# Two attention and feed-forward layers on one core: keys and values made before later queries, the passes of the opening reordered, VectorE's share of the softmax given out by another rule

## Chip, core and metric

One core of a Trainium2 chip. The metric is the device time of one execution in microseconds. A profile's span is the time from the first to the last instruction, about 1.8 us less. All timed runs and profiles named here are in the fast state. A ratio is the mean of one kernel's fast runs over the mean of the other's in the same rounds, so it is not quite the ratio of the medians quoted beside it. In the profiles PE is TensorE (matmuls) and PEld its weight loads, ACT is ScalarE, DVE VectorE and POOL GpSimd; ACTIVATE is the ScalarE instruction that computes exponentials. PSUM is the memory that the matmuls here write; a score tile fills one bank of it. PEclk is the granted clock of TensorE, 1.00 being full; a stretch of half clock is one that the profile records at 0.5.

## The reference, cut to what matters

```python
# 2048 rows of 448, bfloat16; 16 heads of 28; hidden width 1792
x = x + attention(layernorm(x), wqkv, wo)        # full softmax, no mask
x = x + mlp(layernorm(x), w1, b1, w2, b2)        # relu(h)**2
x = x + attention(layernorm(x), wqkv, wo)        # the same weights again
x = x + mlp(layernorm(x), w1, b1, w2, b2)
```

A score tile in this document is 128 keys x 512 columns (two key blocks for 256 queries of one head); there are 1024 a layer, 2048 in all. Every one needs an exponential.

## The kernel before

The kernel doesn't fix its instruction order by hand. While the program is built, a small planner simulates the engines with given durations and priorities, and emits instructions in the order that comes out. A number in it can therefore move work anywhere. The order is fixed when the kernel runs.

```python
BB = 0.85
CUT0 = (0, 2, 4, 8, 12, 16)
LEAD = 60                     # no VectorE tile before this group of scores
V_LATE = 3.0
LAT = {"PE": 0.22, "ACT": 0.22, "DVE": 0.10, ...}   # planner's latencies, us
...
# row statistics of a layer norm, with the duration that the planner assumes
o = Op("DVE", 0.80, fn, deps=deps)
...
# may a score tile be taken from ScalarE and given to VectorE?
def apart(i, now, us, soon=SOON):
    ...
    if pl.load(SPAN, "DVE") > (BB if l == 0 and qb == len(blocks[0]) - 1
                               or l == 1 and units[i][0] < bridged else BUSY):
        return None
    return j
...
# one group of scores: three banks of PSUM for one ACTIVATE
if bank_free(o.start) and next_at(js[-1] + 1):
    j = apart(at[0], o.start, us)            # a fourth tile, in a bank of its own
elif len(us) == 3 and THIRD:
    own = False
    j = apart(at[0], o.start, us[:2], 0.0)   # VectorE takes the third bank
...
# TensorE repeats score matmuls where the plan sees room, so that it isn't idle
for i in list(range(4)) * (again + 1):
    ...
```

A tile that VectorE takes is computed with six instructions (one read from PSUM, four polynomial steps, one power of two). "Chain" below is what follows the attention of 256 rows: output projection, layer norm, feed-forward, and in layer 0 the keys, values and queries of layer 1. The two banks that aren't score buffers serve the chains, the accumulation of the attention output, and the fourth tiles.

The softmax here doesn't subtract the row's maximum and nothing guards it: scores larger than these inputs give would overflow.

## Time and profile before

| | before |
|---|---|
| median of the first 3 runs | 905.57 us |
| ScalarE: three-tile and two-tile ACTIVATEs | 592 and 76 |
| tiles on VectorE | 120 |
| first exponential starts, last one ends | 12.04, 883.44 us |
| after the last exponential | 20.2 us |

The prediction shows the lines and reads them.

### The profile page before, as it was taken

The page shows a single profiled execution, that of the slowest core. Times are in us where ns is not written, and L with a number is a line of the kernel's source. Part 1 is how long each engine was busy: PE and PEld are TensorE (multiplying, and loading weights), DVE is VectorE, ACT ScalarE, POOL GpSimd, SP SyncE. Part 2 cuts the span into 40 slices and gives each one's busy share as a digit, 9 for nine tenths or more (in the row PEclk, how much of TensorE's full clock was granted, in tenths as well). Part 3 has the DMA queues.
Part 4 walks back from the last instruction along what each step waited for, and adds up shares of the span by engine and source line. Part 5 has one row for each costly group of instructions (what it writes and reads, how often), then busy time and mean ns, then how long its engine had stood idle before and what let it go on. Part 6 is the DMA issues. An engine that isn't in the chain of part 4 may idle for free.

```text
span 903.7 us, 29597 instructions
## 1 busy us (share of the span) xinstructions
PE 833.2 (92%) x13089; PEld 464.8 (51%) x13089; DVE 779.4 (86%) x1595; ACT 876.9 (97%) x688; POOL 42.7 (5%) x100
## 2 busy tenths in 40 slices
PE   7999989899999999998999999988999999999998
PEld 4555545455454555545545454544454545545566
DVE  7845789999998999988888988989999999989864
ACT  6999999999999999999999999999999999999992
POOL 4100000000000000000000000000000000000000
PEclk9999999999999999999999999999999999999999
DMA  6200010000000000000000000011000000000100
GB/s 202 95 3 2 2 38 22 15 8 15 9 14 14 15 13 10 14 9 7 3 1 2 2 2 2 2 40 38 24 15 19 14 25 8 25 16 17 29 6 22
DMA packets 32990, 18.47 MB, mean 20 GB/s; under 512 B 17499, under 2 KB 32412, under 8 KB 32861
## 3 DMA queue, kind: packets, MB, share of 16 engines
q1 hardware_dynamic: 32860, 16.58, 6.4%
q8 instruction: 102, 1.67, 0.8%
q14 instruction: 28, 0.22, 0.1%
HBM read 14.26 MB, written 2.07 MB: 18 GB/s over the span
## 4 chain that ended last, share of the span: by engine, by line
ACT 66%; PE 14%; issue 13%; DVE 5%; DMA 1%; POOL 0%; SPq 0%; POOLq 0%; ACTq 0%
ACT pt L805 66%; PE mt L532 6%; PE sc L781 5%; PE oT L950 2%; PE mt L1138 1%; DVE K_sb L878 1%; DMA V_sb<-in_A_wqkv_dram 1%; DVE st L425 1%; DVE xn L498 1%; DVE v_h L878 1%; DVE x_sb L1044 1%; PE sc L532 0%; PE tp L471 0%; DVE K_sb L861 0%; DVE v_i L861 0%
## 5 line engine op out<-in xcount | busy, mean ns | idle before, releaser
L805 ACT ACTIVATE pt<-sc 128x1536 bf16<-128x1536 f32 (+1 forms) x668 | 866.4, 1565 | 2.2 <-PE sc L781 1.7
L781 PE MATMUL sc<-Q_sb,K_sb 32*128 32x256 bf16 (+1 forms) x5966 | 325.9, 265 | 52.7 <-ACT pt L805 47.4
L781 PEld LDWEIGHTS <-K_sb 32*128 32x128 bf16 x6102 | 160.3, 92 | 227.3 <-issue 209.0
L950 PE MATMUL oT<-pt,V_sb 128*32 128x256 bf16 (+1 forms) x4104 | 152.3, 268 | 0.6 <-DVE K_sb L974 0.2
L532 PE MATMUL mt<-xnT,w 128*128 128x256 bf16 (+1 forms) x888 | 118.2, 271 | 3.1 <-DVE r L1087 1.1
L950 PEld LDWEIGHTS <-V_sb 128*32 128x32 bf16 x4352 | 92.4, 96 | 47.5 <-issue 44.5
L878 DVE SCALAR_TENSOR_TENSOR K_sb<-K_sb 128x512 f32<-128x512 uint16 x165 | 113.1, 686 | 0.7
L532 PEld LDWEIGHTS <-w 128*128 128x128 bf16 x952 | 79.0, 98 | 37.6 <-issue 28.9
L878 DVE SCALAR_TENSOR_TENSOR v_h<-v_h,v_i 128x512 f32<-128x512 f32 x130 | 89.1, 685 | 0.4
L1087 DVE TENSOR_SCALAR r<-mt 128x512 bf16<-128x512 f32 x105 | 72.1, 687 | 14.2 <-PE mt L532 14.1
L532 PE MATMUL mt<-w,V_sb 128*128 128x448 bf16 (+1 forms) x288 | 68.6, 352 | 0.0
L447 POOL TENSOR_TENSOR ve<-mv,eps_t 128x2 f32<-128x2 f32 (+1 forms) x34 | 9.5, 280 | 843.7 <-DVE mv L426 778.5
L1138 PE MATMUL mt<-xn,ident 128*128 128x448 bf16 x133 | 45.9, 356 | 2.5 <-DVE x_sb L1044 1.3
L878 DVE SCALAR_TENSOR_TENSOR v_h<-v_i 128x512 f32<-128x512 uint16 x65 | 44.6, 686 | 0.3
L1044 DVE TENSOR_TENSOR x_sb<-x_sb,mt 128x448 bf16<-128x448 bf16 (+1 forms) x64 | 39.1, 611 | 6.3 <-PE mt L532 6.0
L425 DVE BATCH_NORM_STATS2 st<-x_sb 128x6 f32<-128x448 bf16 x64 | 39.6, 619 | 1.0 <-DMA x_sb<-in_A_x_dram 0.6
L532 PEld LDWEIGHTS <-V_sb 128*128 128x128 bf16 x302 | 25.5, 98 | 24.6 <-issue 9.1
L498 DVE TENSOR_SCALAR xn<-x_sb,mv,rstd 128x448 bf16<-128x448 bf16 x64 | 25.3, 420 | 12.9 <-POOL rstd L448 12.5
L532 PE MATMUL mt<-xnT,wq 128*128 128x256 bf16 x248 | 34.0, 274 | 0.0
L532 PE MATMUL mt<-xnT,wk 128*128 128x256 bf16 x240 | 32.9, 274 | 0.6 <-DVE xnT L483 0.4
L1091 DVE TENSOR_TENSOR V_sb<-r 128x512 bf16<-128x512 bf16 (+1 forms) x73 | 30.3, 417 | 2.3 <-ACT r L1085 1.8
L554 DVE CAST K_sb<-mt 128x512 bf16<-128x512 f32 (+1 forms) x31 | 20.8, 672 | 12.7 <-PE mt L532 12.5
(102 smaller groups left out, 790.5 us busy)
## 6 DMA issues: line engine op xcount, KB each, us to landing
rec<-scr SPq DMA_DIRECT2D x56, 128.0 KB
x_sb<-in_A_x_dram SPq DMA_DIRECT2D x8, 224.0 KB
out_dram<-x_sb SPq DMA_DIRECT2D x15, 112.0 KB
w<-in_B_w_dram SPq DMA_DIRECT2D x1, 1568.0 KB
w<-in_B_w_dram SPq DMA_DIRECT2D x1, 1344.0 KB
dn<-oT_sb SPq DMA_DIRECT2D x56, 4.0 KB
scr<-dn SPq DMA_DIRECT2D x56, 4.0 KB
V_sb<-in_A_wqkv_dram SPq DMA_DIRECT2D x1, 672.0 KB
```

Source lines behind the costliest of these rows:

```text
L425: nc.vector.bn_stats(out=st[:, :], in_=x_sb[:, t0 + j, :])
L498: nc.vector.tensor_scalar(out=xn[:, 0:D], in0=x_sb[:, t0 + j, :], scalar1=mv[0][:, j, 0:1], scalar2=ln[j], op0=ALU.subtract, op1=ALU.mult)
L532: nc.tensor.matmul(box["t"][:, c0:c0 + n], lhsT=lhsT() if callable(lhsT) else lhsT, rhs=rhs, start=a, stop=b)
L554: nc.vector.tensor_copy(out=dst, in_=src)
L781: nc.tensor.matmul(dst[k][:, i * nt * P:(i + 1) * nt * P], lhsT=K_sb[l][rows, g, (kb + i) * P:(kb + i + 1) * P], rhs=Q_sb[rows, g, t0 * P: ...
L805: t = nc.scalar.activation(out=pt[:, 0:n], in_=gbuf[gi]["sc"][:, 0:n], func=AF.Exp, scale=float(np.log(2.0)) * 2.0 ** -FRAC)
L878: nc.vector.scalar_tensor_tensor(out=box["h"], in0=box["f"] if begin else box["h"], scalar=b, in1=box["f"], op0=ALU.add, op1=ALU.mult)
L950: nc.tensor.matmul(box["t"][DHP * hh:DHP * hh + DHP, 0:n], lhsT=V_sb[l][:, kb + i, 4 * g + hh, :], rhs=p[:, c0:c0 + n], start=begin and kb ...
L1044: nc.vector.tensor_tensor(out=x_sb[:, tb, lo:hi], in0=x_sb[:, tb, lo:hi], in1=t[:, 0:hi - lo], op=ALU.add)
L1087: nc.vector.tensor_scalar(out=r[:, 0:w], in0=t[:, 0:w], scalar1=0.0, scalar2=None, op0=ALU.max)
L1091: nc.vector.tensor_tensor(out=h[:, 0:w // n, :], in0=r, in1=r, op=ALU.mult)
L1138: nc.tensor.matmul(t[:, 0:D], lhsT=ident[:, :], rhs=xns[0][:, 0:D], start=True, stop=True)
```

## The change

The intent: make all of layer 0's keys and values before the queries of later blocks; keep the normalized rows of blocks 2 to 5 in layer 1's key memory, which is still empty, so that they don't occupy the three row buffers; let VectorE take tiles early; and hold it back where the chains are behind a line of progress. The core of the diff:

```diff
-BB = 0.85
+LINES = ((280, 1312, 8.0), (1440, 2040, 7.0))
+MARGIN = 4.0
+LOW = 0.6
-CUT0 = (0, 2, 4, 8, 12, 16)
+OPENING = ((0, 0, 2), (0, 2, 4), (1, 0, 4), (0, 4, 8), (1, 4, 8), (0, 8, 12), (0, 12, 16), (1, 8, 16))
+OWN3 = 0
-LEAD = 60
+LEAD = 20
-LAT = {"PE": 0.22, "ACT": 0.22, ...}
+LAT = {"PE": 0.25, "ACT": 0.22, ...}
-        o = Op("DVE", 0.80, fn, deps=deps)
+        o = Op("DVE", 0.74, fn, deps=deps)
-            box["x"] = xtp.tile([P, NDC, QR], DT.bfloat16, name="xnT")
+            box["x"] = xtp.tile(...) if place is None else place
+   # in first_block: place=K_sb[1][:, :, (blk - 2) * QR:(blk - 1) * QR] if 2 <= blk <= 5 else None
             def queries():
+                if l == 0 and t0 >= 4:
+                    yield Op("-", 0.0, None, deps=[("V", 0, tb) for tb in range(NTB)])
+    def behind(i):
+        l = 0 if i < LINES[0][1] else 1
+        a, b, n = LINES[l]
+        return done[l] < (min(i, b) - a) / (b - a) * n * per[l] - MARGIN
-        if pl.load(SPAN, "DVE") > (BB if l == 0 and ... else BUSY):
+        if pl.load(SPAN, "DVE") > (LOW if behind(i) else BUSY):
-                if bank_free(o.start) and next_at(js[-1] + 1):
+                if OWN3 and bank_free(o.start) and next_at(js[-1] + 1):
# cut: priorities of VectorE tiles, two more limits on which tile VectorE may take,
# three more planner durations, counting of chain progress, waits that protect the rows lent to layer 1's key memory
```

More of the change, by code (lines that the diff above doesn't have):

```diff
@@ L53 @@
 V_PRIO = 6.0
-V_LATE = 3.0
+V_LATE = 3.6
+V_LAST = 1.8
+V_AGE = 5
+OWN3 = 0
+FIRST = 90
+V_FIRST = 9.2
 V_WAIT = 5.0
@@ L109, in __init__ @@
         self.need, self.got, self.more = need, [], 0.0
-LAT = {"PE": 0.22, "ACT": 0.22, "DVE": 0.10, "POOL": 0.15, "DMA": 2.0, "-": 0.0}
+LAT = {"PE": 0.25, "ACT": 0.22, "DVE": 0.10, "POOL": 0.15, "DMA": 2.0, "-": 0.0}
 class Planner:
@@ L426, in fn, with layernorm @@
             nc.vector.bn_aggr(out=mv[0][:, j, :], in_=st[:, :])
-        o = Op("DVE", 0.80, fn, deps=deps)
+        o = Op("DVE", 0.74, fn, deps=deps)
         mv[1].append(o)
         return o
-    def layernorm(t0, nt, deps_of, early=False, mv=None):
+    def layernorm(t0, nt, deps_of, early=False, mv=None, place=None):
         if mv is None:
@@ L448, in rsqrt @@
                 nc.gpsimd.tensor_tensor(out=rstd[:, a:b], in0=ve[:, a:b], in1=mhalf[:, a:b], op=ALU.pow)
-            rs = Op("POOL", 0.95 if early else 0.6, rsqrt, deps=[mv[1][b - 1]], sets=[("rs", t0 + a)] if early else ())
+            rs = Op("POOL", 0.95, rsqrt, deps=[mv[1][b - 1]], sets=[("rs", t0 + a)] if early else ())
             rss += [rs] * (b - a)
@@ L454, in take @@
         def take(e):
-            box["x"] = xtp.tile([P, NDC, QR], DT.bfloat16, name="xnT")
-        own_xt = Op("DVE", 0.0, take, acq=R_xt)
+            box["x"] = xtp.tile([P, NDC, QR], DT.bfloat16, name="xnT") if place is None else place
+        own_xt = Op("DVE", 0.0, take, acq=R_xt if place is None else None)
         yield own_xt
@@ L611, in queries @@
             def queries():
+                if l == 0 and t0 >= 4:
+                    yield Op("-", 0.0, None, deps=[("V", 0, tb) for tb in range(NTB)])
                 for a in qs:
                     yield from turned(*a)
-                yield Op("DVE", 0.0, None, deps=[last], rel=own_xt)
+                yield Op("DVE", 0.0, None, deps=[last], rel=own_xt if own_xt.res else None)
             if l == 0:
@@ L622, in first_block @@
         gate = [] if GATE[blk] is None else [GATE[blk]]
-        xnT, own_xt, ends = yield from layernorm(2 * blk, 2, lambda j: [("x", blk // 2, blk % 2), *gate, *([("xT", TILES)] if blk == 1 and XT else [])], early)
+        xnT, own_xt, ends = yield from layernorm(2 * blk, 2, lambda j: [("x", blk // 2, blk % 2), *gate, *([("xT", TILES)] if blk == 1 and XT else [])], early,
+                                            place=K_sb[1][:, :, (blk - 2) * QR:(blk - 1) * QR] if 2 <= blk <= 5 else None)
         yield from qkv(0, 2 * blk, 2, xnT, own_xt, ends, early)
@@ L632, in add_passes @@
                     passes.append((l, qb, g, range(lo, hi), lo == 0, hi == NTB))
-    for cut in zip(CUT0, CUT0[1:]):
-        if cut == (0, 2):
-            add_passes(0, [0], cut)
-        elif cut == (2, 4):
-            add_passes(0, [0], cut)
-            add_passes(0, [1], (0, 4))
-        else:
-            add_passes(0, [0, 1], cut)
+    for qb, lo, hi in OPENING:
+        add_passes(0, [qb], (lo, hi))
     for qb in range(2, len(blocks[0])):
@@ L666 @@
     held = [0]
+    done = [0.0, 0.0]
+    per = [1.6 + 7 + 5.6 + 6.0, 1.6 + 7 + 5.6]
+    def behind(i):
+        l = 0 if i < LINES[0][1] else 1
+        a, b, n = LINES[l]
+        return done[l] < (min(i, b) - a) / (b - a) * n * per[l] - MARGIN
     pending = [0]
@@ L693, in apart @@
             j = js[0] if js else j
+        if passes[units[j][0]][0] != passes[us[0][0]][0]:
+            return None
         if held[0] + 1 > min(sum(r.n for r in pd_free(units[k])) for k in (i, j)):
@@ L697, in apart @@
             return None
-        if pl.load(SPAN, "DVE") > (BB if l == 0 and qb == len(blocks[0]) - 1 or l == 1 and units[i][0] < bridged else BUSY):
+        if pl.load(SPAN, "DVE") > (LOW if behind(i) else BUSY):
             return None
@@ L821, in pd_free @@
             return (R_pd[0], *(R_pd[1:5] if qb <= 6 else R_pd[3:5]))
+        if len(norm_done.get((0, len(blocks[0]) - 1), ())) < G:
+            return tuple(R_pd[:1])
         return tuple(R_pd[:1] + R_pd[6:]) if hidden_left[0] else tuple(R_pd[:1] + R_pd[5:])
@@ L866, in a_unit @@
         yield c
-        pl.spawn(lambda now: V_LATE if now > c.end + V_WAIT else V_PRIO, a_rest(gi, c, box, unit, (b0, b1, b2, b3)))
+        pl.spawn(lambda now: V_LAST if e_now[1] - gi >= V_AGE else V_LATE if now > c.end + V_WAIT else V_PRIO if gi > FIRST else V_FIRST, a_rest(gi, c, box, unit, (b0, b1, b2, b3)))
     def a_rest(gi, c, box, unit, bs):
@@ L1011, in spread @@
                                   in_=res["t"][DH::DHP, 0:n])
-            d1 = Op("DMA", 0.5, spread, deps=[oe], lat=0.5)
+            d1 = Op("DMA", 0.5, spread, deps=[oe], lat=1.0)
             yield d1
@@ L1034, in mul @@
                                     in1=box["r"][:, 0:n], op=ALU.mult)
-        m = Op("DVE", 0.1 + n / 960, mul, deps=[r, oTn_of[l, qb][1]], rel=oe)
+        m = Op("DVE", 0.13 + n / 930, mul, deps=[r, oTn_of[l, qb][1]], rel=oe)
         yield m
@@ L1059, in chain @@
                 post=[lambda a, j=j: stats(mv, t0, j, [a])])
+            done[l] += 0.8
         yield Op("DVE", 0.0, None, deps=[a], rel=own_on)
         xnT, own_xt, ends = yield from layernorm(t0, nt, None, mv=mv)
-        own_h = Op("DVE", 0.0, None, acq=R_h[l])
+        own_h = Op("DVE", 0.0, None, acq=R_h[l], deps=[("Q", 0, g, t0 + 4) for g in range(G)] if l == 0 and qb < 4 else ())
         yield own_h
@@ L1099, in chain @@
                 relu, 0.70, [*ends, ("w1",)], True, post=[then], acq=R_r)
+            done[l] += w / 512
             for i in range(len(fcs)):
@@ L1116, in chain @@
                           (lambda a, store=store: Op("DMA", 0.5, store, deps=[a]))])
+            done[l] += 2.8
         yield Op("DVE", 0.0, None, deps=[a], rel=own_h)
@@ L1121, in chain @@
             yield from qkv(1, t0, nt, *xt2)
+            done[0] += 6.0
     def heat():
```

## The prediction

> **What bounds the kernel now.** I first read the page's busy shares and the chain that ended last, then the groups by form, then ScalarE's timeline of the opening, then busy time by stretch.
>
> ```profile
> PE 833.2 (92%) x13089; PEld 464.8 (51%) x13089; DVE 779.4 (86%) x1595; ACT 876.9 (97%) x688; POOL 42.7 (5%) x100
> ...
> ACT 66%; PE 14%; issue 13%; DVE 5%; DMA 1%; POOL 0%; SPq 0%; POOLq 0%; ACTq 0%
> ```
>
> ScalarE (ACT) is busy 97% of the span and holds two thirds of the chain. Its work is the softmax's exponentials. Three score tiles of 128x512 (or two) are one ACTIVATE:
>
> ```profile
> L805 ACT ACTIVATE pt<-sc 128x1536 bf16<-128x1536 f32 x592 | 812.9, 1612 | 2.2 <-PE sc L781 1.7 <-PE oT L950 0.2
> L805 ACT ACTIVATE pt<-sc 128x1024 bf16<-128x1024 f32 x76 | 87.4, 1197 | 0.0
> ```
>
> The columns are count, busy time, mean ns and idle time before. Neighbours overlap, so the means can't be summed. I took the distance between the ends of consecutive ACTIVATEs from the trace's records: the median is 1343 ns where the later one has three tiles and 917 ns where it has two. The difference, 426 ns, is one tile; what is left, 1343 - 3 x 426 = 65 ns (or 63 with 426.7 a tile), is the fixed cost of one. Check: 592 x 1.343 + 76 x 0.917 = 864.7, against 866.4 us busy on the page. Of the 2048 tiles, 592 x 3 + 76 x 2 = 1928 go to ScalarE; the other 120 are a polynomial on VectorE.
>
> ```profile
> core 0: us, PE busy (x) PEld busy (x) DVE busy (x) ACT busy (x) POOL busy (x), PEclk, DMA share, GB/s
> ...
> 12.00:28.00 16.00, 13.55 (x165) 7.86 (x166) 13.04 (x28) 13.63 (x13) 6.34 (x13) 1.00 0.68 211
> 28.00:60.00 32.00, 31.06 (x443) 17.46 (x444) 22.20 (x48) 32.00 (x25) 3.67 (x8) 1.00 0.03 11
> 60.00:330.00 270.00, 249.81 (x4010) 140.82 (x4004) 234.98 (x475) 269.42 (x208) 7.56 (x20) 1.00 0.05 14
> 330.00:470.00 140.00, 130.12 (x1945) 69.58 (x1942) 124.11 (x241) 139.92 (x109) 6.87 (x16) 1.00 0.03 8
> 470.00:700.00 230.00, 211.83 (x3225) 114.46 (x3222) 208.18 (x424) 229.69 (x181) 7.28 (x18) 1.00 0.05 14
> 700.00:883.00 183.00, 170.21 (x3063) 96.52 (x3061) 159.48 (x329) 183.00 (x144) 5.40 (x10) 1.00 0.07 18
> 883.00:904.00 21.00, 16.98 (x204) 12.51 (x200) 9.33 (x22) 4.41 (x8) 0.93 (x2) 1.00 0.06 19
> ```
>
> Busy time by stretch shows ScalarE full from 28 to 883 us: even the boundary between the layers (330 to 470) costs it 0.08 us. So the span is three pieces: 12.0 us before the first exponential, 871.4 from its start to the end of the last (883.4), and 20.3 of tail. The middle holds 864.7 of exponentials at their regular distance and 6.7 of anything else. Most of that 6.7 is in the opening:
>
> ```profile
> 12.04 2.79 ACT L805 ACTIVATE pt<-sc 128x1536 bf16<-128x1536 f32 x2 [0.19 <-PE sc L781]
> 14.72 0.54 ACT L580 CAST V_sb<-sc 128x448 bf16<-128x448 f32 x1
> 15.32 2.79 ACT L805 ACTIVATE pt<-sc 128x1536 bf16<-128x1536 f32 x2
> 19.05 1.45 ACT L805 ACTIVATE pt<-sc 128x1536 bf16<-128x1536 f32 x1 [0.93 <-PE sc L781]
> 20.79 0.37 ACT L552 CAST K_sb<-sc 128x256 bf16<-128x256 f32 x1 [0.30 <-PE sc L532]
> 21.55 0.53 ACT L580 CAST V_sb<-mt 128x448 bf16<-128x448 f32 x1 [0.38 <-PE mt L532]
> 22.08 4.14 ACT L805 ACTIVATE pt<-sc 128x1536 bf16<-128x1536 f32 x3
> 26.86 0.38 ACT L548 ACTIVATE Q_sb<-mt 128x256 bf16<-128x256 f32 x1 [0.65 <-PE mt L532]
> ```
>
> Between the first and the ninth exponential stand four evictions, 0.54 + 0.37 + 0.53 + 0.38 = 1.82 us, and idle times of 0.93 + 0.30 + 0.38 + 0.65 = 2.26. After 28 us all stalls that I find in the records sum to about 2 us, none over 0.43.
>
> **What the Trainium skill says.** "ScalarE: Activation LUTs", section What ACT_TABLE_LOAD costs, gives an ACTIVATE with immediate operands 186 ns + 0.833 ns per element, and an overlap of about 93 ns back to back, so 93 ns fixed. The trace agrees on the element (426 / 512 = 0.833 ns), and has 63 to 65 ns fixed; I use the trace. "Advanced Engine Details and Errata", section Bank Collisions, lets ScalarE and VectorE read PSUM at full rate at once when they are in different banks. The 76 two-tile ACTIVATEs, 75 of them beside a VectorE read of the third bank of the same buffer, keep to 917 ns, so it agrees. "SBUF — State Buffer", section Who interferes with whom, says that a VectorE tensor_scalar in a two-port mode and a GpSimd instruction exclude each other for a whole instruction. The trace fits: at 14.56 us two normalizations take 2.13 us together (420 ns each elsewhere) beside GpSimd memsets of 0.94 and 1.60 us.
>
> **The change part by part.** I compared the instruction order of both built programs.
>
> *Exponentials.* Before, 45 VectorE tiles had a bank of their own beside a full three-tile ACTIVATE, and 75 were the third bank of a score buffer. Now all are the third bank, and there are 126. ScalarE has 556 three-tile and 127 two-tile ACTIVATEs: 556 x 3 + 127 x 2 = 1922 tiles. Six fewer tiles save 6 x 0.427 = 2.56 us; 683 instead of 668 instructions cost 15 x 0.063 = 0.95. Directly: 556 x 1.343 + 127 x 0.917 = 863.2, so **-1.5 us** out of 864.7. VectorE starts at the 20th ACTIVATE instead of the 60th, which fills the stretch of 28 to 60 us where it was busy only 22.2 of 32; that stretch gets 8 tiles where it had one. The rest of the program, under the hold-back by chain progress, gives one back net.
>
> *VectorE's load.* A tile there is a read of 0.69, four steps of 0.68 and one of 0.42 us; issued back to back they stand 0.60 and 0.34 apart, so 5 x 0.60 + 0.34 = 3.3 us. Six more are +20 us; joining two pass pieces of the opening removes 4 additions of partial sums (32 to 28), -1.4. VectorE goes to about 798 us, 88%. Still under ScalarE.
>
> *Opening.* The instructions before the first exponential are the same, so 12.0 us stay. Then come five exponentials in a row, two key evictions and one of values (0.37 + 0.37 + 0.53 = 1.27 us), then exponentials without end. One eviction of 0.55 us moves from ScalarE to VectorE, and the query eviction with its wait (0.38 + 0.65 = 1.03) leaves ScalarE too. Against it, VectorE now does one row statistic (0.79), one value eviction (0.61) and one partial sum (0.41) more before it copies the transposed rows of block 1, on which the sixth exponential waits. Some of this hides in the GpSimd collision (2.13 - 0.72 = 1.4 us). I put the sixth exponential at 21 to 22 us, against 22.08. Choosing half a microsecond earlier, and 1.03 for the query: **-1.5 us**.
>
> *Early VectorE tiles.* They begin at group 19 while keys of rows 6 and 7 are due at group 22, on a VectorE that still makes them[...]. I allow **+0.5 us** for a wait there. Keeping rows in layer 1's key memory frees row buffers but removes no instruction: the order shows as many projections and transposes as before, only with another source tile.
>
> *Boundary and tail.* ScalarE had no wait at the boundary to win back. The last exponential is still a two-tile one, and the listings of VectorE and ScalarE after it match line for line: 20.3 us stay. For a fuller VectorE I allow **+0.5 us** more of small PE waits.
>
> Sum: -1.5 - 1.5 + 0.5 + 0.5 = -2.0; 905.57 - 2.0 = 903.6, and since the author's tuning should have removed some of the 2 us of small stalls, I say 903.3.
>
> **The rivals.** *A shared score bank held too long.* A score buffer is free only once both engines have read it, and shared reads go from 75 to 126. Were each late by 0.1 us, 51 x 0.1 = 5 us would come back and the time would be about 908. Against it: in the trace before, VectorE's read ended a median 0.6 us before the ACTIVATE that shares the buffer, the latest 0.16 us after, and none was followed by idle ScalarE. *VectorE becomes the bound.* At 88% in sum, parts are fuller: 90.5% in 470 to 700 now. If chains fall behind, layer 1's last keys come late and ScalarE idles at the boundary: 2 to 6 us, so 905 to 909. Against it: the hold-back exists for this, and ten percent stays free. *The opening stalls.* If early tiles delay the keys of later blocks, 2 to 4 us are lost before 60 us: 905 to 907. *It opens better than I think.* If all 4.1 us but the 1.27 of evictions go, and small stalls too, the time is about 900.5.
>
> **Range and chances.** Exponentials are counted and hardly uncertain (0.3 us). The opening is uncertain by 1.5 us either way, the later stalls by 1 to 2, more on the slow side. So 8 in 10 for 901.0 to 905.9. Two per cent is 18 us: more than everything that isn't an exponential or the unchanged ends, so faster by that much is almost excluded, and slower needs 26 ns more on each of 683 ACTIVATEs (18 / 683): 1% each.
>
> **What would show it right or wrong.** Right: 556 and 127 ACTIVATEs at the same 1343 and 917 ns, busy near 864.8; VectorE near 798; ScalarE without idle time from the sixth exponential on but for about 2 to 3 us in all; a tail of 20.3 us. The step on the opening is wrong if ScalarE's sixth exponential starts after 22.5 us, or if idle time stands near the 20th to 30th. The step on shared banks is wrong if score matmuls wait for VectorE's read, or the two-tile distance exceeds 917. All is wrong if ScalarE idles for microseconds near the layer boundary, or the tail is not 20.3.

## The result, and the profile after

903.79 us (median of 4 runs, 902.81 to 904.10), against 906.14 before in the same rounds; the ratio is 0.9969 (95%: 0.9949 to 0.9989). A later call on another occasion gave 903.20 against 906.39, ratio 0.9962. The prediction was 903.3, with a range of 901.0 to 905.9.

The page of the changed kernel: first busy time by engine, then the chain that ended last.

```profile
PE 833.8 (92%) x12828; PEld 459.2 (51%) x12828; DVE 798.2 (89%) x1628; ACT 874.6 (97%) x702; POOL 41.8 (5%) x100
...
ACT 72%; issue 13%; PE 9%; DVE 5%; DMA 1%; SPq 0%; ACTq 0%; DVEq 0%
```

VectorE rose by 18.8 us and ScalarE stayed at 97%, with more of the chain. The groups by form:

```profile
L819 ACT ACTIVATE pt<-sc 128x1536 bf16<-128x1536 f32 x556 | 776.8, 1652 | 4.1 <-PE sc L795 3.9
L819 ACT ACTIVATE pt<-sc 128x1024 bf16<-128x1024 f32 x127 | 146.0, 1235 | 0.0
```

These are the two counts of the prediction; the idle time before them nearly doubled, from 2.2 to 4.1 us. The distances between the ends of ACTIVATEs are unchanged, 1343 and 917 ns as medians. ScalarE's timeline in the opening (start, duration, what, count, and in brackets the idle time before):

```profile
11.16 5.52 ACT L819 ACTIVATE pt<-sc 128x1536 bf16<-128x1536 f32 x4 [0.19 <-PE sc L795]
17.59 1.45 ACT L819 ACTIVATE pt<-sc 128x1536 bf16<-128x1536 f32 x1 [0.91 <-PE sc L795]
19.32 0.37 ACT L559 CAST K_sb<-sc 128x256 bf16<-128x256 f32 x1 [0.28 <-PE sc L539]
19.75 0.37 ACT L559 CAST K_sb<-mt 128x256 bf16<-128x256 f32 x1
20.51 0.53 ACT L587 CAST V_sb<-mt 128x448 bf16<-128x448 f32 x1 [0.38 <-PE mt L539]
20.94 49.45 ACT L819 ACTIVATE pt<-sc 128x1536 bf16<-128x1536 f32 x38
```

From the start of the first exponential to that of the ninth it is 13.78 us, against 15.16 before (12.04 to 27.20): 1.38 less. Of these, 0.25 us are gained up to the sixth (9.78 against 10.03), and 1.13 after it, where the query eviction with its wait stood. After the sixth there is no break at all up to 70 us, though VectorE's tiles start here. The surprise is later:

```profile
400.05 2.97 ACT L819 ACTIVATE pt<-sc 128x1536 bf16<-128x1536 f32 x2 [0.28 <-PE sc L795]
404.30 1.45 ACT L819 ACTIVATE pt<-sc 128x1536 bf16<-128x1536 f32 x1 [1.28 <-PE sc L795]
406.09 4.14 ACT L819 ACTIVATE pt<-sc 128x1536 bf16<-128x1536 f32 x3 [0.34 <-PE sc L795]
```

ScalarE waits for score matmuls, and busy time by stretch suggests why: the granted clock of TensorE, PEclk, falls. (It is the first number after the five engines.) The first line is the stretch that the prediction called the boundary between the layers; there ScalarE was idle for 0.08 us before the change and is now for 2.60.

```profile
core 0: us, PE busy (x) PEld busy (x) DVE busy (x) ACT busy (x) POOL busy (x), PEclk, DMA share, GB/s
330.00:470.00 140.00, 129.02 (x1902) 69.31 (x1901) 121.79 (x231) 137.40 (x110) 5.39 (x12) 0.98 0.03 8
...
390.00:395.00 5.00, 4.25 (x90) 2.84 (x89) 5.00 (x11) 5.00 (x5) 1.06 (x4) 1.00 0.09 29
395.00:400.00 5.00, 3.51 (x64) 2.14 (x62) 5.00 (x10) 4.77 (x4) 0.00 (x0) 0.78 0.00 0
400.00:405.00 5.00, 5.00 (x41) 2.16 (x36) 2.68 (x6) 3.60 (x3) 0.00 (x0) 0.54 0.02 4
405.00:410.00 5.00, 5.00 (x95) 2.69 (x94) 1.68 (x4) 4.66 (x4) 0.00 (x0) 1.00 0.08 23
```

The clock records place one stretch of half clock at 397.8 us, 6.8 us long. I sum what each ACTIVATE after 30 us took beyond its regular distance (excesses under about 0.05 us left out) and call it late waits: 1.96 us before, 3.94 after, of which 2.4 in this stretch.

The accounts of the two profiles, 903.7 - 901.8 = 1.9 us: exponentials 864.7 - 863.2 = 1.5; opening 1.4; an earlier first exponential 0.9; a tail shorter by 0.1; less 2.0 of late waits. The pieces sum to 1.9.

### The profile page after: what moved, and what is told of

Same layout as the page of the kernel before. It is cut to its first block, busy times and chain, and to the rows that moved or that the text cites. A ratio compares the mean times of both kernels' runs of the same rounds, so it can differ in the third digit from the quotient of the medians.

```text
span 901.8 us, 29143 instructions
## 1 busy us (share of the span) xinstructions
PE 833.8 (92%) x12828; PEld 459.2 (51%) x12828; DVE 798.2 (89%) x1628; ACT 874.6 (97%) x702; POOL 41.8 (5%) x100
## 4 chain that ended last, share of the span: by engine, by line
ACT 72%; issue 13%; PE 9%; DVE 5%; DMA 1%; SPq 0%; ACTq 0%; DVEq 0%
ACT pt L819 72%; PE mt L539 4%; PE sc L795 2%; PE oT L966 1%; DVE st L432 1%; PE sc L539 1%; DMA V_sb<-in_A_wqkv_dram 1%; DVE K_sb L894 1%; DVE v_h L894 0%; DVE xn L505 0%; DVE x_sb L1060 0%; PE mt L1158 0%; DVE mv L433 0%; DVE v_i L877 0%; DVE K_sb L877 0%
## 5 line engine op out<-in xcount | busy, mean ns | idle before, releaser
L795 PEld LDWEIGHTS <-K_sb 32*128 32x128 bf16 x5840 | 156.6, 92 | 234.2 <-issue 204.2
L894 DVE SCALAR_TENSOR_TENSOR v_h<-v_h,v_i 128x512 f32<-128x512 f32 x142 | 96.9, 682 | 0.5
L877 DVE TENSOR_SCALAR v_i<-sc 128x512 int32<-128x512 f32 x71 | 48.6, 685 | 9.9 <-PE sc L795 9.3
L894 DVE SCALAR_TENSOR_TENSOR v_h<-v_i 128x512 f32<-128x512 uint16 x71 | 48.6, 685 | 0.5
L877 DVE TENSOR_SCALAR K_sb<-sc 128x512 int32<-128x512 f32 x55 | 37.6, 684 | 5.6 <-PE sc L795 5.4
L988 DVE COPY oT_sb<-oT 128x256 f32<-128x256 f32 (+1 forms) x48 | 19.0, 396 | 17.0 <-PE oT L966 16.9
L539 PE MATMUL mt<-wo,oTn 128*128 128x448 bf16 x128 | 31.6, 355 | 0.1
```

What stands on the lines that cost most here:

```text
L539: nc.tensor.matmul(box["t"][:, c0:c0 + n], lhsT=lhsT() if callable(lhsT) else lhsT, rhs=rhs, start=a, stop=b)
L795: nc.tensor.matmul(dst[k][:, i * nt * P:(i + 1) * nt * P], lhsT=K_sb[l][rows, g, (kb + i) * P:(kb + i + 1) * P], rhs=Q_sb[rows, g, t0 * P: ...
L877: t = nc.vector.tensor_scalar(out=box["i"], in0=two(src), scalar1=EXP_BIAS, scalar2=EXP_LOW, op0=ALU.add, op1=ALU.max)
L894: nc.vector.scalar_tensor_tensor(out=box["h"], in0=box["f"] if begin else box["h"], scalar=b, in1=box["f"], op0=ALU.add, op1=ALU.mult)
L988: nc.vector.tensor_copy(out=dst, in_=src)
```

## The experiments

"Ninth" is the start of the ninth exponential after that of the first; "exponentials" is three-tile count x 1.343 + two-tile count x 0.917 (and 0.490 for one tile), from the built program and the distances. Runs named a_ edit the changed kernel, b_ and bo_ the kernel before. All results were correct. The three calls (after_again to a_split, b_stats to a_best, a_own3 to a_oldorder) ran on three different chips and had 906.39, 906.17 and 906.01 us for the kernel before, so medians of different calls differ by 0.4 us from that alone.

| run | median us | ratio to before | exponentials | ninth | late waits | tail |
|---|---|---|---|---|---|---|
| before (39 runs beside the last call) | 906.01 | 1 | 864.7 | 15.16 | 1.96 | 20.2 |
| after_again | 903.20 | 0.9962 | 863.2 | 13.78 | 3.84 | 20.2 |
| a_heat | 901.72 | 0.9951 | 863.2 | 15.41* | 1.73 | 20.2 |
| a_pool | 902.67 | 0.9964 | 863.2 | 13.81 | 4.20 | 20.2 |
| a_split | 908.65 | 1.0033 | 869.4 | 15.41* | 5.04 | 20.2 |
| b_stats | 909.76 | 1.0039 | 865.4 | 13.79 | 1.91 | 24.1 |
| b_opening | 917.87 | 1.0124 | 863.5 | 16.48* | 12.59 | 23.0 |
| a_lead60 | 906.54 | 1.0004 | 866.6 | 13.78 | 0.47 | 23.0 |
| a_best | 900.49 | 0.9938 | 863.2 | 12.78 | 1.72 | 20.2 |
| a_own3 | 904.20 | 0.9982 | 862.7 | 13.78 | 4.86 | 19.9 |
| a_bb | 906.99 | 1.0008 | 863.6 | 13.78 | 3.36 | 24.5 |
| bo_own0 | 909.44 | 1.0036 | 866.1 | 17.55* | 0.84 | 22.5 |
| a_oldorder | 906.63 | 1.0003 | 865.3 | 13.78 | 2.93 | 21.9 |

(* this profile had a stretch of half clock in the opening as well.)

My theory after the result: ScalarE's count and the opening give about 3 us, and a stretch of half clock takes 2 us of it back (run 2 limits the second part to the two profiles). The rivals: the waits near 400 us are waits for VectorE's tiles; the gain in the opening comes from other parts of the change than I thought.

**1. The changed kernel again.**

> The changed kernel once more, so that the others of this call can be compared with it on one chip. Theory A (the clock dip belongs to the change's own instruction order): its profile shows again a granted clock near 0.54 between 400 and 405 us of the span, and about 3.2 us of ScalarE idle time between 376 and 407 us. Theory B (the dip was chance): a mean clock of 1.00 and less than 1 us of idle time there. The first exponential, at 12.04 us in the kernel before and 11.16 in the changed one, moves with the landing of the first weights if it is chance: anywhere from 11 to 12.2.

The half clock is there again, at 397.4 us and 6.8 us long, with similar waits (2.0 us of idle ScalarE between 376 and 408 us, where I had expected 3.2): it belongs to the program. The first exponential started at 12.15 us this time. Over all profiles it lies between 11.06 and 12.15 with the same ScalarE instructions before it. The chain of each profile begins with the transfer of the first weights, which ended at 7.72 us in the kernel before, at 6.84 in the changed one and at 7.83 this time. So the 0.9 us of the first comparison were the landing of that transfer, by chance.

**2. More score matmuls before the half clock.** The plan stays (the trace lists the same 702 ScalarE and 1628 VectorE instructions in the same order); only the number of repeats that are emitted changes (repeats overwrite the scores with themselves).

```diff
-                for i in list(range(4)) * (again + 1):
+                more = {300: 1, 301: 1, 302: 1, 303: 2}.get(gi, 0)
+                for i in list(range(4)) * (again + 1 + more):
```

> The changed kernel with its plan kept and five more repeats of score matmuls, one each in groups 300, 301 and 302 and two in group 303, just before the dip. Theory A (TensorE was too idle from 393 to 398 us, its clock was cut to a half for 6.8 us, and ScalarE waited for slow score matmuls): clock 1.00 throughout, the idle time of ScalarE between 398 and 407 us falls from about 2.3 us to under 0.3, and the time falls by 2.0 to 2.5 us against the changed kernel, to about 901.5. Rival (ScalarE waits there for VectorE's late tiles, and the clock only accompanies it): the waits stay and the time changes by less than 0.7 us.

```profile
390.00:395.00 5.00, 4.94 (x90) 2.76 (x89) 4.97 (x11) 5.00 (x5) 1.06 (x4) 1.00 0.11 30
395.00:400.00 5.00, 3.89 (x87) 3.03 (x87) 4.96 (x11) 5.00 (x5) 0.00 (x0) 1.00 0.00 2
400.00:405.00 5.00, 4.78 (x80) 2.74 (x76) 4.62 (x9) 4.93 (x5) 0.00 (x0) 1.00 0.02 4
405.00:410.00 5.00, 4.93 (x93) 2.63 (x90) 1.68 (x5) 5.00 (x5) 0.00 (x0) 1.00 0.09 26
```

The clock stays at 1.00, and of 2.4 us of waits after 398 us 0.2 are left, with VectorE at least as full as before. The rival falls: the waits came from the half clock. The median fell by 1.5 us (1.0 by the ratios), less than I expected, and this profile shows why: a stretch of half clock of 3.4 us came up in the opening (at 18.7 us), and the ninth exponential was 1.6 us late. Five of the six runs have a mean clock of 1.00 and a median of 901.68; the sixth, with 0.998, took 903.39.

That gives a way to read the spread of all runs. The 28 runs of the kernel before in this call, sorted by mean clock: 6 at 1.000 have a median of 904.66 us, 9 at 0.998 of 905.96, 7 at 0.996 of 906.84, 6 at 0.994 of 908.16. Half clock for 3.4 us is 0.002 of the span and goes with a microsecond or so. The changed kernel was never at 1.000 in its 11 runs; in the 7 of this call it had 902.75 at 0.998 and 904.01 at 0.996, 3.2 and 2.8 us less than the kernel before at equal clock. Without any half clock, it is 901.68 (this run) against 904.66: 3.0 us.

So half clock did not come with the change. Of these 28 runs of the kernel before 22 had some by their mean clock, though the profile that the prediction read had none, and the median of all 28 lies 1.7 us above that of the six without. The changed kernel's lies 1.5 us above that of this run's five. The half clock explains why the two profiles differ by only 1.9 us; from the difference of the medians it takes next to nothing. What belongs to the change is the stretch near 400 us.

**3. The memset that blocks a normalization.** In the changed kernel a normalization at 14.4 us took 1.39 us beside a GpSimd memset from 14.08 to 15.67; the value eviction behind it was late, TensorE waited 1.17 us for it, and ScalarE's fifth exponential 0.91.

```diff
-        yield Op("POOL", 1.6, lambda e: nc.gpsimd.memset(w1[DL:P, 3, :], 0.0), sets=("w10",))
-        yield Op("POOL", 0.2, lambda e: nc.gpsimd.memset(sel[:], 0.0), deps=[("K", 0, 1, 3)])
+        yield Op("POOL", 1.6, lambda e: nc.gpsimd.memset(w1[DL:P, 3, :], 0.0), deps=[("K", 0, 1, 3)], sets=("w10",))
+        yield Op("POOL", 0.2, lambda e: nc.gpsimd.memset(sel[:], 0.0))
```

> The changed kernel with the GpSimd memset of 1.6 us (rows of w1) put after the first block's keys instead of at 14.1 us; the ScalarE instructions are the same, 556 and 127. Theory (this memset blocks a normalization on VectorE, which took 1.39 us instead of 0.40; the value eviction behind it made TensorE wait 1.17 us and ScalarE's fifth exponential 0.91 us): the normalization takes 0.4 us, the idle time before the fifth exponential falls by 0.5 to 0.9 us and the time by as much, 0.1 per cent. Rival (the next wait takes its place: keys of block 1 are just as late): the idle time moves to the sixth exponential and the time stays within 0.3 us.

```profile
11.18 6.88 ACT L819 ACTIVATE pt<-sc 128x1536 bf16<-128x1536 f32 x5 [0.19 <-PE sc L795]
...
20.56 0.53 ACT L587 CAST V_sb<-mt 128x448 bf16<-128x448 f32 x1 [1.40 <-PE mt L539]
```

The wait before the fifth exponential went, and the wait before the value eviction grew from 0.38 to 1.40 us. The memset now ran at 17.51 us, beside the next normalization, which took 1.67 us. The ninth exponential gained nothing (13.81 us), nor did the ratio (0.9964 against 0.9962). The rival was right here, but by a second collision of the same kind.

**4. Cutting ACTIVATEs in two**, to measure the fixed cost that the prediction charges for more ACTIVATEs.

```diff
-                t = nc.scalar.activation(out=pt[:, 0:n], in_=gbuf[gi]["sc"][:, 0:n], ...)
+                cut = 1024 if n == 1536 and 100 <= gi < 580 and gi % 4 == 0 else n
+                for lo, hi in ((0, cut), (cut, n)):
+                    if lo < hi:
+                        t = nc.scalar.activation(out=pt[:, lo:hi], in_=gbuf[gi]["sc"][:, lo:hi], ...)
```

> The changed kernel with 98 of its three-tile ACTIVATEs (every fourth group from 100 to 579, where it has three tiles) cut into one of two tiles and one of one tile, plan unchanged. Theory (each ACTIVATE costs 63 ns beside 427 ns a tile, and ScalarE is the bound): 98 x 0.063 = +6.2 us against the changed kernel, near 910, and the distance between ends is 917 ns for the first part and about 490 ns for the second. Rival (the fixed cost is hidden when the same bank buffer is read on, or ScalarE has slack): under +3 us.

The 98 one-tile parts end 490 ns after their first parts (median, mean 490.04). So one, two and three tiles take 490, 917 and 1343 ns: 427 a tile and 63 fixed. By ratio the kernel is 1.0033 / 0.9962 = 1.0071 times the changed one, 6.4 us; by medians 5.5; at equal clock 5.1 (907.89 against 902.75 at 0.998) and 5.3 (909.28 against 904.01 at 0.996). So the count's 6.2 is nearly all there, ScalarE is the bound, and the distances give 63 ns as the price of an ACTIVATE; up to 1 us that isn't there at equal clock stays unexplained. This profile has four stretches of half clock; that slower exponentials leave TensorE less to do would fit, but wasn't tested.

**5. One planner number alone.** I looked for the line of the diff that gives the opening of the changed kernel, by building variants. It is this one:

```diff
-        o = Op("DVE", 0.80, fn, deps=deps)
+        o = Op("DVE", 0.74, fn, deps=deps)
```

> The kernel before with one number of the change's: the planner is told 0.74 instead of 0.80 us for a row statistic on VectorE. By the built program this alone gives ScalarE the changed kernel's opening (five exponentials in a row, two key evictions, one of values, then exponentials without end), but 588 three-tile, 82 two-tile and 1 one-tile ACTIVATEs: 1929 x 0.427 + 671 x 0.063 = 865.4 us, 0.6 more than before. Theory (the opening's gain of 1.3 us comes from this number, not from keys and values first or the reordered passes): from the first to the ninth exponential it takes about as long as in the changed kernel, 13.8 us instead of 15.2, and the time falls by 0.5 to 1 us against before. Rival (the order of the passes makes the opening faster): 15.2 us stay, and the time rises by 0.6.

The ninth exponential comes 13.79 us after the first, as in the changed kernel and with the old order of passes: the gain of the opening is this number's. But the time rose by 3.6 us, where I expected a fall of 0.5 to 1. The profile has the reason: 24.1 us after the last exponential instead of 20.2. My sum had taken the tail for fixed. It isn't, once the plan moves.

**6. What the title names, alone.** The kernel before with OPENING, the rows in layer 1's key memory and the wait of queries for values.

```diff
-    for cut in zip(CUT0, CUT0[1:]):
-        ...
+    for qb, lo, hi in OPENING:
+        add_passes(0, [qb], (lo, hi))
+   # and: place=K_sb[1][...] for blocks 2 to 5, queries() waits for all values
```

> The kernel before with only what the title of the change puts first: queries of blocks 2 to 7 after all values, rows of blocks 2 to 5 in layer 1's key memory, and the reordered passes. Start of the VectorE tiles, hold-back and durations stay. 587 and 82 ACTIVATEs: 863.5 us, 1.2 less than before; ScalarE's opening stands as before (two exponentials, values, three, ...). Theory (these parts make nothing faster by themselves, they free VectorE early and so allow tiles): 1.2 us faster than before through the count, the ninth exponential 15.2 us after the first as before. Rival (keys and values first spares ScalarE waits): the ninth exponential comes a microsecond sooner, and the time falls by 2 us or more.

On the time both were wrong, badly: 917.87 us, 1.2% slower. ScalarE's timeline has one line that explains nearly all of it:

```profile
584.89 6.40 ACT L802 ACTIVATE pt<-sc 128x1536 bf16<-128x1536 f32 x5 [10.64 <-PE sc L778]
```

Between 574 and 585 us the score matmuls stand behind the keys of layer 1's last rows. VectorE comes to the statistics of these rows at 575.67 us, behind tiles; TensorE waits 3.29 us for their normalization; then follow transposes and projection, most of it at half clock (from 577.9 us, 6.8 us long). The opening isn't tested cleanly here: the ninth exponential came 16.48 us after the first, but with a half clock of 3.4 us from 18.1 us, and such a stretch made the ninth 1.6 us late in a_heat. Run 11 tests it.

**7. The same without banks of their own for VectorE tiles.**

```diff
-                if bank_free(o.start) and next_at(js[-1] + 1):
+                if 0 and bank_free(o.start) and next_at(js[-1] + 1):
```

> The run with the reordered passes alone, and own banks given up besides; all other numbers as before the change. 563 and 120 ACTIVATEs: 866.1 us, 2.6 more than with own banks. In the built order layer 1's last keys come 3 to 6 groups ahead instead of within 3. Theory (own banks cause the boundary wait): the idle time of 10.6 us near 585 falls under 1 us, and the time falls by about 8 us against that run, to 907 to 911 by the tail that comes. Rival (the boundary wait is the reordered passes' doing, or missing hold-back): it stays over 5 us.

The long wait is gone (late waits 0.84 us in all) and the time fell by 8.4 us although the exponentials take 2.6 us more. So with this order of passes it is the fourth tiles that let layer 1's last keys come too late; the hold-back line isn't needed to cure it. That they do so by sitting in the chains' banks is argued, not shown: without them VectorE also has four tiles fewer (119 instead of 123), and gets the others at other times. Run 8, where the number of tiles stays (125 against 126), says that it isn't the number. Against the profile of the kernel before it is 4.1 us longer: 1.4 of exponentials, 2.3 of tail, 2.4 of an opening with half clock (from 16.6 us, 6.8 us long), less 1.1 of late waits and 0.9 of an earlier start.

**8. Fourth tiles put back into the changed kernel.**

```diff
-OWN3 = 0
+OWN3 = 1
```

> The changed kernel with VectorE tiles allowed again in a bank of their own beside a full three-tile ACTIVATE. 584 three-tile, 85 two-tile and 1 one-tile ACTIVATEs: 862.8 us, 0.4 less than the changed kernel. But own banks are those in which the chains of layer 0 compute; in the order of the built program layer 1's last keys (rows 14 and 15) then come within 2 groups of the group that needs them, against 8 to 11 groups ahead in the changed kernel, much as in the run with the reordered passes alone, where ScalarE stood still for 10.6 us there. Theory (own banks are given up to keep the chains ahead at the layer boundary): an idle time of 2 to 11 us near 575 to 595 us, and 2 to 11 us slower than the changed kernel. Rival (only the count matters): no long wait there, 0.4 us faster.

```profile
578.79 2.37 ACT L819 ACTIVATE pt<-sc 128x1024 bf16<-128x1024 f32 x2 [3.03 <-PE sc L795]
```

3.0 us at the layer boundary, in the predicted place and at the low end of the predicted size. Against the changed kernel it is 1.0 us slower by medians, less than the 2 to 11 expected; against the run without the half clock near 400 us (which this plan doesn't have either), 904.09 - 901.68 = 2.4 us at a clock of 1.00. OWN3 = 0 gives up 0.4 us of ScalarE time for this.

**9. The start of VectorE tiles.**

```diff
-LEAD = 20
+LEAD = 60
```

> The changed kernel with VectorE's tiles from the 60th group on, as before, instead of from the 20th. 564 and 119 ACTIVATEs, 1930 tiles: 866.6 us, 3.4 more than the changed kernel (118 VectorE tiles instead of 126). Theory (ScalarE's count of tiles sets the time): 3.4 us slower than the changed kernel, about 906.5, if the clock dip near 400 us stays; 1 to 2 us less if the new plan has no dip. Rival (early tiles cost VectorE work that the opening needs, so starting late gives part back): less than 1.5 us slower, and fewer idle times of ScalarE before 60 us.

906.54 us, 3.3 more than the changed kernel, as the count said. But partly by luck: the exponentials cost 3.4 more and the tail 2.8 more, while the late waits are 3.4 less, with no half clock in this profile. At a clock of 1.00 it is 906.62 against 901.68, and 3.4 + 2.8 - 1.3 (late waits against those of a_heat) = 4.9 accounts for it.

**10. The old rule of holding back, in the changed kernel.**

```diff
-        if pl.load(SPAN, "DVE") > (LOW if behind(i) else BUSY):
+        if pl.load(SPAN, "DVE") > (0.85 if l == 0 and qb == len(blocks[0]) - 1 or l == 1 and units[i][0] < bridged else BUSY):
```

> The changed kernel with the old rule for holding VectorE tiles back (VectorE's load under 0.85 in the last query block of layer 0 and before the bridge of layer 1) instead of the lines of chain progress. 557 and 126 ACTIVATEs: 863.6 us, 0.4 more. In the built order layer 1's last keys come 7 to 11 groups ahead. Theory (with own banks given up, the order has room enough at the boundary under either rule): no wait over 1 us near 575 to 595, within 1.5 us of the changed kernel, beyond what another clock dip or another tail adds. Rival (the new rule is what prevents the boundary wait): several us of idle time there.

No wait over 1.03 us anywhere, and none near the last keys; still 3.8 us slower by medians, and 4.2 at a clock of 1.00 (905.90 against a_heat's 901.68). The difference is in the tail: 24.5 us instead of 20.2. After the last exponential 28 VectorE instructions and 20.2 us of TensorE work are left, against 22 and 16.4 in the changed kernel. Chains of layer 1 were left for the end. So in this version the lines of progress serve the end of the program, not the boundary.

**11. The old order of passes, in the changed kernel.**

```diff
-OPENING = (..., (0, 8, 12), (0, 12, 16), (1, 8, 16))
+OPENING = (..., (0, 8, 12), (1, 8, 12), (0, 12, 16), (1, 12, 16))
```

> The changed kernel with the opening's passes in their old order (keys 8 to 12 for both query blocks, then 12 to 16). 561 and 122 ACTIVATEs, 1927 tiles: 865.3 us, 2.1 more. ScalarE's first fifteen exponentials are the same. Theory (the order of the passes acts only through VectorE's time, so through the number of its tiles): the ninth exponential 13.8 us after the first, and 2.1 us slower than the changed kernel in the middle; the clock dip may be gone (up to 2 us back) and the tail may change, as in other replanned versions. Rival (the order avoids waits of ScalarE before 60 us): idle times appear between 25 and 90 us.

The ninth exponential didn't move (13.78 us) and there is no wait between 25 and 90 us: in this plan the order of the passes acts through the number of VectorE tiles. At a clock of 1.00 it takes 905.75, 4.1 us more than a_heat: 2.1 of exponentials, 1.7 of tail; the rest I didn't follow.

**12. A version that beats both.** The repeats of run 2, and the memset at the end of GpSimd's set-up.

```diff
+                more = {300: 1, 301: 1, 302: 1, 303: 2}.get(gi, 0)
-        yield Op("POOL", 1.6, lambda e: nc.gpsimd.memset(w1[DL:P, 3, :], 0.0), sets=("w10",))
+        # last in late_setup:
+        yield Op("POOL", 1.6, lambda e: nc.gpsimd.memset(w1[DL:P, 3, :], 0.0), deps=[("V", 0, 3)], sets=("w10",))
```

> The changed kernel with the five extra repeats before the clock dip, and the GpSimd memset of w1 moved behind all other set-up and the values of row block 3 (it ran at 18 us in the last trial and blocked another normalization; now it should run near 22 us, where VectorE reads only PSUM). ScalarE's work stays 863.2 us. If the lock on the shared port holds the opening up, both waits go: no idle time before the fifth exponential, 0.3 to 0.4 us before the value eviction, and the sixth exponential starts 8.7 to 9.0 us after the first instead of 9.8. With the dip gone, 2.3 to 3 us faster than the changed kernel: about 900.7. If the next wait takes over again: as the run with the repeats alone, 901.7.

```profile
11.10 6.88 ACT L820 ACTIVATE pt<-sc 128x1536 bf16<-128x1536 f32 x5 [0.19 <-PE sc L796]
...
19.45 0.53 ACT L587 CAST V_sb<-mt 128x448 bf16<-128x448 f32 x1 [0.39 <-PE mt L539]
19.88 21.18 ACT L820 ACTIVATE pt<-sc 128x1536 bf16<-128x1536 f32 x16
```

900.49 us (5 runs, 900.38 to 901.55), 0.6% less than before in the same rounds and less than the changed kernel (in another call) by 2.7 us by medians, or 0.9938 / 0.9962 = 0.9976, 2.2 us, by ratios. The memset ran from 18.67 us, earlier than I expected, but behind the two normalizations, which took 0.38 and 0.39 us. Both waits are gone and the sixth exponential starts 8.78 us after the first. ScalarE's and VectorE's instructions stand in the same order as in the changed kernel. So in this plan the memset beside a normalization is shown to have held the opening up by 1.0 us; that a shared port is the reason is the account of the page that the prediction names, which fits.

## Why the prediction was right, point by point

- **Exponentials, -1.5 us: right.** 556 and 127 at 1343 and 917 ns; run 4 measured the fixed cost by itself.
- **Opening, -1.5 us: right in size (1.38), but split otherwise, and its start was off by chance.** I gave half a microsecond to the stretch up to the sixth exponential and 1.03 to the query; they were 0.25 and 1.13. I kept 12.0 us for the first exponential; it varies by 1.1 us from run to run. What I didn't see is which line makes the opening: not keys and values first, nor the passes, but the planner's 0.74 us for a row statistic (runs 5 and 11).
- **Early VectorE tiles, +0.5: wrong, it was 0.** 38 exponentials follow one another through that stretch. The "8 tiles where it had one" are counted in groups up to the 60th, not in the stretch of 28 to 60 us: in the traces 3 tiles start there, and 9 before 100 us, against 0 and 1 before the change.
- **Late waits, +0.5 and then 0.3 off for tuning: mis-sized.** They grew by 2.0 us, to 3.94, and the half clock near 400 us is 2.4 of these. None of my rivals had TensorE's clock; the column that shows it was 1.00 throughout before, and I read no more from it. Without it (a_heat) the late waits are 1.73 against 1.96. Then the change is worth 3.0 us at equal clock, what the first two terms promise.
- **"All is wrong if ScalarE idles for microseconds near the layer boundary": it did.** In the stretch of 330 to 470 us that the prediction means, its idle time went from 0.08 to 2.60 us. The cause was not the one behind the sign, chains that are late, but the half clock (run 2).
- **The total, 903.3: partly luck.** For waits of all kinds the prediction allowed 0.7 us net. In the profiles they cost 2.0, and an earlier start by chance gave 0.9 back. In the medians of the later call both kernels carry about 1.5 us of half clock; the prediction took its base, 905.57, from such a median without knowing of it.
- **Tail of 20.3 and shared banks: right.** 20.15 us. VectorE's read of the shared bank ended at most 0.15 us after its ACTIVATE, and no idle ScalarE followed. The rival of chains that fall behind didn't come in the changed kernel; runs 6 and 8 show that it does come where the fourth tiles stay.
- **VectorE near 798 us:** 798.2.

Why so large a diff moves so little: its parts hold each other up. The early start brings eight tiles and the order of passes five, each worth 0.4 us. With these in place the fourth tiles must go (put back, they cost 2.4 us) and a line of progress must hold VectorE back (without it the tail costs 4.3); that a full VectorE is the link between these is my reading of runs 8 and 10. Parts taken alone made the kernel slower, by 3.6 and 11.7 us. What stays open: why a replanned tail lands at 20, 22 or 24 us I followed only for a_bb.

## What to carry to other kernels

Where one engine is full, count its instructions in the built program and take their regular distance from the trace: that term held to 0.1 us. Then look for what isn't in the count. Read the column of TensorE's clock in the profile, and the mean clock of the timed runs too: a profile at 1.00 can stand for a minority of the runs, as it did here (6 of 28), and a small gain is best compared at equal clock. A few useless matmuls at the right place removed one stretch of half clock (run 2). And when an edit moves a memset or a tile, look where it lands: run 3's wait moved one collision on, and run 6's 1.2 us of saved exponentials came with a wait of 10.6 us at the next layer.

## What the Trainium skill lacked or had wrong

- "TensorE: Matmul & The Clock Gate", Part 1: its table puts the half clock after at least one idle window of about 3.4 us; further down the page says that frequent short idle times can do it too, but nowhere how busy TensorE has to be. In the changed kernel the 3.4 us before the cut had 2.00 us of matmul records, 59% busy, and no gap over 0.51 us. Over all profiles the cuts came behind windows 18 to 68% busy. No threshold comes out of this: a_oldorder was cut behind a window 68% busy and not behind one 60% busy (some matmul records can be missing). The page's length of the window is confirmed (3.41 us or twice that), and half clock is the one low state seen. Within one profile the stretches of half clock begin whole multiples of 3.413 us apart (a_split: 18.426, 226.639, 404.132 and 861.518 us); where they fall differs from run to run, which fits the page's free-running window.
- The same page gives the cost of the half clock in TensorE's own time, not what it costs a kernel bound elsewhere: here 904.66 us of the kernel before at a mean clock of 1.000 and 908.16 at 0.994, about a microsecond for each 3.4 us of half clock.
- "ScalarE: Activation LUTs", What ACT_TABLE_LOAD costs: about 93 ns fixed for back-to-back ACTIVATEs by its figures; 63 ns here (490, 917 and 1343 ns for 512, 1024 and 1536 elements). Its 0.833 ns an element is confirmed.
- "SBUF — State Buffer", Who interferes with whom: nothing wrong. The page gives no duration; here a normalization of 0.38 to 0.40 us took 1.39 and 1.67 us beside a memset of 1.59 us.
